# The next pair's first score product placed between two heads' transposes of probabilities

## The chip, the core and the metric

The kernel runs on one core of a Trainium2 chip. The metric is device time in microseconds (us), the median of several runs. The core has TensorE (PE, with its weight loads as PEld), VectorE (DVE), ScalarE (ACT), GpSimd (POOL) and the queue engine SyncE (SP).

## The reference

Attention with sinks and a window (batch 4, 8 heads, 768 positions, head size 64), then a dense layer with a clipped quadratic activation, then an expert-choice layer of 8 experts:

```python
scores = scale * np.matmul(q, k.transpose(0, 1, 3, 2))
keep = is_sink | in_window              # pos < n_sink (4), or 0 <= i - j < window (128)
scores = np.where(keep, scores, -1000000000.0)
scores = scores - np.max(scores, axis=-1, keepdims=True)
a = np.exp(scores)
a = a / (np.sum(a, axis=-1, keepdims=True) + 1e-09)
x = np.matmul(a, v)                     # heads joined: 3072 tokens x 512
...
h = x @ w_in                            # 512 -> 2048
g = np.where(pos, h, np.where(neg, 0.0, (h + beta) ** 2 / (4.0 * beta)))
x = g @ w_out                           # 2048 -> 512
...
logits = x @ w_gate                     # then tokens go to 8 experts of 384 places
out[mask] = np.maximum(x[mask] @ w1[e], 0.0) @ w2[e]
```

Inputs and outputs are float32.

## The kernel before

The 3072 tokens are worked in 12 blocks of 256 (three blocks to a batch entry, so every third one is a "first" block without a block before it). A block's attention is done by pairs of heads, four pairs to a block. Blocks 0 and 1 run in plain float32 (attn_steps_f32); the ten others (attn_steps) split most operands into a high part, rounded to the fast float32 form, and a low part, the remainder.

For a pair of heads the steps are: load_kq and load_v (DMA from SP); trans_k (keys turned on VectorE, the high part ks by ACT on line 303, the low part by VectorE on line 304, columns of the sinks on line 309); trans_q (queries turned on line 431, high part sq by ACT on line 317, low part ql by VectorE on line 318); for each head hh and half u of the block a score product s_hh_u (lines 335 and 336, two products into a PSUM bank; VectorE adds the mask and takes the maximum on line 338, ACT the exponential and its sum on line 340); norm for each head (VectorE sums and reciprocals on lines 345 and 346, GpSimd multiplies the probabilities pr on line 354, or on 349 and 351 in a first block); ptrans for each head (TensorE transposes of the probabilities, line 373, copied out as pt by ACT on 375 and VectorE on 376); strans (the sinks' part of both heads, lines 363 to 366; not in a first block); pv for each head (products with the values, line 392, copied out as xa on 398 and 399); and split (GpSimd, ACT and GpSimd, lines 408 to 413), which writes the pair's quarter of the dense layer's input xh and xl.

ks, sq and ql have one buffer each, so the next pair's can be written only when the last score product of a pair, s11, has read them. Score products, transposes and value products take turns in three PSUM banks.

The order of these steps is a list in `pipeline`: one string per pair, in which a bare name is the pair at hand, "+" the next pair, "*" the one after it, "^" the one after that. `attn` spreads a pair's steps evenly over its time; steps in `idle` take none of it, the others one unit. The dense layer's steps are spread over the same time: hid (12 products of line 634 from xh, xl, then u, gh and gl by lines 642 to 646) and proj (12 products of line 659). `Plan.run` calls all of them in the order of these times, and the Tile scheduler then orders the instructions on each engine: it mostly keeps that order, and moves an instruction behind others that it reckons to be ready sooner. So in TensorE's row a step of 12 products of the dense layer stands between most steps of the attention, and a step that moves in the list moves against these.

After the attention, from about 785 us on, the routing and the experts follow.

Of the kernel before, what the change touches and what calls it, by code (L numbers as in the profile page):

```python
# [74 lines left out]
class Kernel:  # L75
# [524 lines left out]
    def pipeline(self, pairs):  # L600

        idle = {"load_kq", "load_v", "trans_k", "trans_q", "norm0", "norm1", "split_v", "sinks", "split"}

        def steps(order, now, nxt, far, last):
            of = {"": now, "+": nxt, "*": far, "^": last}
            found = [(of[s.rstrip("abcdefghijklmnopqrstuvwxyz_0123456789")], s.lstrip("+*^")) for s in order.split()]
            return [(0.0 if s in idle and s not in d.get("on_pe", ()) else 1.0, d[s]) for d, s in found if d and d[s]]

        out = [steps("load_kq load_v trans_k trans_q +load_kq split_v sinks +load_v s00 s01 norm0 s10 s11 norm1 "
                     "+trans_k +trans_q *load_kq",  # L610
                     pairs[0], pairs[1], pairs[2], None)]
        for now, nxt, far, last in zip(pairs, *(pairs[i:] + [None] * i for i in (1, 2, 3))):
            out.append(steps("ptrans0 ptrans1 strans +s00 +s01 +norm0 pv0 +s10 +s11 +norm1 "
                             "*trans_k *trans_q ^load_kq "
                             "pv1 +split_v +sinks *load_v split", now, nxt, far, last))
        return out
# [765 lines left out]
def tile_sink_window_attention__moe__expert_choice(ctx, tc, q, k, v, n_sink, window, w_in, w_out, wg, w1, w2, out):  # L1382
# [10 lines left out]
    def pipeline(general):  # L1393
        with ExitStack() as c0:
# [72 lines left out]
            plan.run()  # L1467

    pipeline(False)
    flag = nc.values_load(K.flag[0:1, 0:1], min_val=0, max_val=1)  # L1470
    with tc.If(flag):
        with ExitStack() as c0:
            K.attn_general(c0.enter_context, xg)
        pipeline(True)
# [32 lines left out]
```

## Time and profile before

| | us |
|---|---|
| median of 3 runs | 1190.5 (1190.31 to 1192.92) |
| the profiled execution | 1191.5 |
| its span, first to last instruction | 1189.7 |
| TensorE busy | 1113.0 (94%) |
| VectorE busy | 862.4 (72%) |
| ScalarE busy | 701.3 (59%) |
| GpSimd busy | 487.4 (41%) |

Busy shares are averages over stages with different limits. A wait in the trace is the idle time of an engine ahead of an instruction, with what ended it. Products are pipelined and their ends are modelled, so steps on TensorE are best measured from start to start. Times of day are counted from the span's start.

### The profile page before, as it was taken

The numbers are of one execution on the slowest core, as the hardware profiler recorded it, in microseconds if no ns is written. First come the engines' busy times: TensorE is split into PE (matmuls) and PEld (weight loads), VectorE is DVE, ScalarE is ACT, GpSimd is POOL, SyncE is SP. The second block draws the span as 40 slices with busy tenths as digits, with TensorE's granted clock in tenths as the row PEclk, the third lists the DMA queues.
The fourth block names the chain that finished last, engine by engine and source line by source line (L and its number), as shares of the span: only waits on it lengthen the run. The fifth ranks groups of instructions, "written<-read, shape, count | busy, mean of one in ns | idle before, by whom it ended". The sixth has DMA issues, their size and how long they took to land.

```text
span 1189.7 us, 24247 instructions
## 1 busy us (share of the span) xinstructions
PE 1113.0 (94%) x8256; PEld 1027.3 (86%) x8256; DVE 862.4 (72%) x2578; ACT 701.3 (59%) x1602; POOL 487.4 (41%) x588
## 2 busy tenths in 40 slices
PE   5998989999999999999999999999699999999995
PEld 3788878999999999999999999999578888888994
DVE  6778788878677887776778787655788787878330
ACT  5877677666667666666667666642335434443651
POOL 1336645444545445544545554541222222322321
PEclk9999899999999999999999999999799999999998
DMA  4556422323232223222222322000677667666861
GB/s 112 142 163 169 145 51 59 70 42 63 46 63 41 40 54 60 47 46 55 34 57 46 69 46 62 3 19 1 186 196 194 196 169 204 198 191 191 226 177 39
DMA packets 241926, 118.11 MB, mean 99 GB/s; under 512 B 196096, under 2 KB 220672, under 8 KB 241792
## 3 DMA queue, kind: packets, MB, share of 16 engines
q1 hardware_dynamic: 233200, 86.58, 28.5%
q0 software_dynamic: 8592, 29.89, 10.7%
q8 instruction: 67, 1.10, 0.4%
q14 instruction: 67, 0.55, 0.2%
HBM read 86.00 MB, written 13.11 MB: 83 GB/s over the span
## 4 chain that ended last, share of the span: by engine, by line
PE 58%; DVE 13%; issue 10%; ACT 6%; POOL 5%; DMA 4%; SPq 2%; DVEq 0%; POOLq 0%; ACTq 0%
PE hp L634 15%; PE up L659 14%; PE hp L1056 8%; PE us L1083 7%; PE xp L392 2%; PE tp L373 2%; PE sc L335 1%; DVE u L642 1%; PE sc L336 1%; POOL pr L354 1%; SPq L427 1%; DVE ks L304 1%; PE pk L957 1%; ACT u L643 1%; PE sc L517 1%
## 5 line engine op out<-in xcount | busy, mean ns | idle before, releaser
L646 POOL TENSOR_TENSOR gl<-u,gh 128x256 fp32r<-128x256 f32 x192 | 150.8, 785 | 204.6 <-ACT gh L645 163.7
L659 PE MATMUL up<-woh,gl 128*128 128x256 f32 (+1 forms) x576 | 168.5, 293 | 2.9 <-POOL gl L646 2.9
L659 PE MATMUL up<-wol,gh 128*128 128x256 f32 (+1 forms) x576 | 165.5, 288 | 0.8 <-POOL wol L249 0.8
L659 PE MATMUL up<-woh,gh 128*128 128x256 f32 x576 | 164.9, 287 | 0.0
L643 ACT ACTIVATE u<-u,half 128x256 f32<-128x256 f32 x192 | 97.7, 509 | 88.3 <-DVE u L642 84.4
L634 PE MATMUL hp<-xh,wil 128*128 128x256 f32 x768 | 133.5, 293 | 5.2 <-POOL wil L249 3.1
L634 PE MATMUL hp<-xl,wih 128*128 128x256 f32 x768 | 127.3, 286 | 2.6 <-POOL xl L413 2.3
L634 PE MATMUL hp<-xh,wih 128*128 128x256 f32 x768 | 126.2, 285 | 0.0
L634 PEld LDWEIGHTS hp<-xh,wil 128*128 128x128 f32 x768 | 108.3, 192 | 8.8 <-POOL wil L249 4.1
L659 PEld LDWEIGHTS up<-woh,gl 128*128 128x128 f32 x576 | 110.4, 192 | 4.3 <-POOL gl L646 3.7
L659 PEld LDWEIGHTS up<-wol,gh 128*128 128x128 f32 x576 | 110.4, 192 | 1.7 <-POOL wol L249 1.0
L634 PEld LDWEIGHTS hp<-xl,wih 128*128 128x128 f32 x768 | 107.4, 192 | 4.2 <-POOL xl L413 3.8
L659 PEld LDWEIGHTS up<-woh,gh 128*128 128x128 f32 x576 | 110.3, 192 | 0.0
L642 DVE TENSOR_SCALAR u<-hp 128x256 f32<-128x256 f32 x192 | 80.1, 417 | 40.4 <-PE hp L634 32.2
L634 PEld LDWEIGHTS hp<-xh,wih 128*128 128x128 f32 x768 | 107.5, 193 | 0.4 <-issue 0.4
L644 DVE TENSOR_TENSOR u<-hp,u 128x256 f32<-128x256 f32 x192 | 80.6, 420 | 31.8 <-ACT u L643 30.1
L340 ACT ACTIVATE pr<-pr,sm 128x288 f32<-128x288 f32 (+1 forms) x160 | 85.2, 533 | 20.2 <-DVE sm L338 19.7
L354 POOL TENSOR_TENSOR pr<-pr,sm 128x576 f32<-128x576 f32 x56 | 70.0, 1250 | 65.2 <-DVE sm L346 37.3
L645 ACT CAST gh<-u 128x256 fp32r<-128x256 f32 x192 | 77.6, 404 | 27.2 <-DVE u L644 25.0
L1064 ACT ACTIVATE hh<-hp 128x384 fp32r<-128x384 f32 x64 | 31.5, 492 | 104.2 <-PE hp L1056 89.1
L1083 PE MATMUL us<-w2h,hl 128*128 128x512 f32 x192 | 80.8, 421 | 0.0
L376 DVE TENSOR_TENSOR pt<-tp,pt 128x512 fp32r<-128x512 f32 (+1 forms) x80 | 51.4, 647 | 39.6 <-ACT pt L375 39.0
(270 smaller groups left out, 3038.4 us busy)
## 6 DMA issues: line engine op xcount, KB each, us to landing
w1r<-in_moe_w_dram SPq DMA_DIRECT2D x32, 512.0 KB, 4.3
w2r<-in_moe_w_dram SPq DMA_DIRECT2D x32, 512.0 KB, 4.7
w2l<-w2r POOLq DMA_DIRECT2D x32, 512.0 KB
qr<-in_q_dram SPq DMA_DIRECT2D x320, 32.0 KB, 2.0
dr<-in_moe_w_in_dram SPq DMA_DIRECT2D x16, 512.0 KB, 4.1
dr<-in_moe_w_out_dram SPq DMA_DIRECT2D x16, 512.0 KB, 3.7
x2d<-ev SPq DMA_DIRECT2D x26, 256.0 KB, 2.2
kr<-in_k_dram SPq DMA_DIRECT2D x112, 48.0 KB, 2.2
```

Source lines behind the costliest of these rows:

```text
L340: nc.scalar.activation(pr, pr, AF.Exp, bias=sm[:, 0, u:u + 1], scale=-1.0, accum_out=sm[:, 1, u:u + 1])
L354: nc.gpsimd.tensor_tensor(out=pr, in0=pr, in1=r.unsqueeze(2).to_broadcast([P, 2, 2 * P + NS]), op=OP.mult)
L376: nc.vector.tensor_tensor(out=pt[:, 1, :n], in0=ps, in1=pt[:, 0, :n].bitcast(F32), op=OP.subtract)
L634: nc.tensor.matmul(ps, w_[:, k, fs], x_[:, k, :], start=(i == 0 and k == 0), stop=(i == 2 and k == 3))
L642: nc.vector.tensor_scalar(u, ps, -1.0, 1.0, op0=OP.max, op1=OP.min)
L643: nc.scalar.activation(u, u, AF.Square, bias=self.half, scale=0.5)
L644: nc.vector.tensor_tensor(out=u, in0=ps, in1=u, op=OP.max)
L645: nc.scalar.copy(gh, u)
L646: nc.gpsimd.tensor_tensor(out=gl, in0=u, in1=gh.bitcast(F32), op=OP.subtract)
L659: nc.tensor.matmul(o, g_[:, ts], self.w_out_part(w_, f)[:, cs], start=(f == fa and i == 0 and (cs.start > 0 or t == 0)), stop=(f == fz - 1 ...
L1056: nc.tensor.matmul(ps, w_[:, k, fs], x_[:, k, :], start=(i == 0 and k == 0), stop=(i == 2 and k == 3))
L1083: nc.tensor.matmul(us[j], h_[:, o], w_[:, f % 2, :], start=(f == 0 and i == 0), stop=(f == nf - 1 and i == 2))
```

## The change

In the string of every pair, the next pair's first score product (+s00) stands between the first and the second head's transposes. The other steps keep their places.

```diff
         for now, nxt, far, last in zip(pairs, *(pairs[i:] + [None] * i for i in (1, 2, 3))):
-            out.append(steps("ptrans0 ptrans1 strans +s00 +s01 +norm0 pv0 +s10 +s11 +norm1 "
+            out.append(steps("ptrans0 +s00 ptrans1 strans +s01 +norm0 pv0 +s10 +s11 +norm1 "
                              "*trans_k *trans_q ^load_kq "
                              "pv1 +split_v +sinks *load_v split", now, nxt, far, last))
```

What this does to the rows of an engine shows in the built program. TensorE, in a pair of block 7 (its last score product starts at 496.76 us in the trace below); the names are xp for value products, tp for transposed probabilities, hp for the dense layer's hidden products, up for its output products, sc for scores. Before:

```order
L392 MATMUL xp<-pt,v_7047 128x256 x2
L373 MATMUL tp<-ident,pr 128x128 x4
L634 MATMUL hp<-xh,wil 128x256 x4
L634 MATMUL hp<-xl,wih 128x256 x4
L634 MATMUL hp<-xh,wih 128x256 x4
L373 MATMUL tp<-ident,pr 128x128 x4
L659 MATMUL up<-woh,gl 128x256
L659 MATMUL up<-wol,gh 128x256
```

and now:

```order
L392 MATMUL xp<-pt,v_7047 128x256 x2
L373 MATMUL tp<-ident,pr 128x128 x4
L634 MATMUL hp<-xh,wil 128x256 x4
L634 MATMUL hp<-xl,wih 128x256 x4
L634 MATMUL hp<-xh,wih 128x256 x4
L659 MATMUL up<-woh,gl 128x256
L659 MATMUL up<-wol,gh 128x256
L335 MATMUL sc<-ks,ql 128x288
L336 MATMUL sc<-ks,sq 128x288
L659 MATMUL up<-woh,gh 128x256
```

The second head's transposes have left their place behind the hidden products, and the score product stands two output products further on; the transposes follow after the other ten output products of that step.

VectorE, same pair, from the copy of the value products over ql to the copies of the transposes. Before:

```order
L399 TENSOR_TENSOR xa<-xp,xa 64x512
L318 SCALAR_TENSOR_TENSOR ql<-qr,sq 128x512
L376 TENSOR_TENSOR pt<-tp,pt 128x512
L642 TENSOR_SCALAR u<-hp 128x256
L376 TENSOR_TENSOR pt<-tp,pt 128x512
L644 TENSOR_TENSOR u<-hp,u 128x256
L366 TENSOR_TENSOR st<-tps,st 64x256
```

and now:

```order
L399 TENSOR_TENSOR xa<-xp,xa 64x512
L318 SCALAR_TENSOR_TENSOR ql<-qr,sq 128x512
L376 TENSOR_TENSOR pt<-tp,pt 128x512
L642 TENSOR_SCALAR u<-hp 128x256
L338 ISA pr,sm<-sc,m_130 128x288
L338 ISA sm 128x1
L644 TENSOR_TENSOR u<-hp,u 128x256
L376 TENSOR_TENSOR pt<-tp,pt 128x512
```

ql stands where it stood; the mask and maximum of the score product have come ahead of the second head's transposed probabilities.

VectorE in a pair of block 5 (its last score product starts at 376.07 us), around ql. Before:

```order
L304 TENSOR_TENSOR ks<-kr,ks 64x3x128
L399 TENSOR_TENSOR xa<-xp,xa 64x512
L318 SCALAR_TENSOR_TENSOR ql<-qr,sq 128x512
L376 TENSOR_TENSOR pt<-tp,pt 128x512
L642 TENSOR_SCALAR u<-hp 128x256
```

and now:

```order
L304 TENSOR_TENSOR ks<-kr,ks 64x3x128
L346 RECIPROCAL sm<-sm 128x2
L309 CAST ks<-sk 128x2x2x32
L318 SCALAR_TENSOR_TENSOR ql<-qr,sq 128x512
L399 TENSOR_TENSOR xa<-xp,xa 64x512
L642 TENSOR_SCALAR u<-hp 128x256
L376 TENSOR_TENSOR pt<-tp,pt 128x512
```

Here the copy of the value products has moved behind ql.

## Rows read from the trace of the kernel before

**Rows 1.** Sums by stretch: busy us and count by engine, granted clock, DMA.

```profile
150.00:290.00 140.00, 130.85 (x1033) 125.15 (x1032) 113.13 (x314) 96.42 (x248) 70.27 (x87) 1.00 0.27 55
290.00:785.00 495.00, 476.04 (x3875) 470.85 (x3874) 372.03 (x1041) 326.83 (x827) 249.95 (x313) 0.99 0.24 48
```

**Rows 2.** Who TensorE's products waited for, 290 to 785 us (sum, times, longest).

```profile
PE tp L373 <- POOL pr L354: 13.9, 10, 2.0
PE hp L634 <- POOL xl L413: 2.3, 2, 1.2
PE hp L634 <- ACT xh L412: 1.5, 4, 0.5
```

**Rows 3.** The same view, 150 to 290 us.

```profile
PE sc L335 <- DVE ql L318: 2.9, 5, 0.9
PE tp L373 <- POOL pr L354: 2.1, 4, 0.9
```

**Rows 4.** TensorE in order of time: start, us, line, names, count, [idle before].

```profile
496.76 0.29 PE L335 MATMUL sc<-ks,ql 128*128 128x288 f32 x1
497.02 0.28 PE L659 MATMUL up<-woh,gl 128*128 128x256 f32 x1
...
498.46 0.40 PE L392 MATMUL xp<-pt,v 128*128 128x256 f32 x2
...
499.05 0.64 PE L373 MATMUL tp<-ident,pr 128*128 128x128 f32 x4
499.45 0.72 PE L634 MATMUL hp<-xh,wil 128*128 128x256 f32 x4
...
503.02 0.74 PE L373 MATMUL tp<-ident,pr 128*128 128x128 f32 x4 [1.91 <-POOL pr L354]
...
508.23 0.29 PE L335 MATMUL sc<-ks,ql 128*128 128x288 f32 x1
```

**Rows 5.** GpSimd in order of time, same stretch: the second head's normalisation.

```profile
501.50 1.47 POOL L354 TENSOR_TENSOR pr<-pr,sm 128x576 f32<-128x576 f32 x1
```

**Rows 6.** VectorE in order of time, same stretch: up to the low query part.

```profile
500.91 1.04 DVE L304 TENSOR_TENSOR ks<-kr,ks 64x384 fp32r<-64x384 f32 x1
501.99 0.68 DVE L399 TENSOR_TENSOR xa<-xp,xa 64x512 f32<-64x512 f32 x1
502.70 0.81 DVE L318 SCALAR_TENSOR_TENSOR ql<-qr,sq 128x512 fp32r<-128x512 f32 x1
```

**Rows 7.** TensorE in order of time, a pair of a first block.

```profile
436.34 0.30 PE L335 MATMUL sc<-ks,ql 128*128 128x288 f32 x1
...
438.41 0.52 PE L373 MATMUL tp<-ident,pr 128*128 128x128 f32 x3
...
442.22 0.33 PE L335 MATMUL sc<-ks,ql 128*128 128x128 f32 x1
```

**Rows 8.** VectorE in order of time, same pair.

```profile
440.32 1.27 DVE L318 SCALAR_TENSOR_TENSOR ql<-qr,sq 128x512 fp32r<-128x512 f32 x1
```

**Rows 9.** TensorE in order of time, first hidden product of a block.

```profile
469.96 0.39 PE L634 MATMUL hp<-xh,wil 128*128 128x256 f32 x1 [0.43 <-ACT xh L412]
...
471.87 0.38 PE L634 MATMUL hp<-xl,wih 128*128 128x256 f32 x1 [1.17 <-POOL xl L413]
```

**Rows 10.** Sums by stretch, TensorE alone: busy, count, granted clock, DMA, GB/s.

```profile
316.30:319.70 3.40, 3.40 (x19) 0.51 0.43 69
504.00:507.40 3.40, 3.40 (x19) 0.50 0.36 58
570.50:573.90 3.40, 3.40 (x31) 1.00 0.33 52
```

**Rows 11.** Line of the low query part: duration in ns, min/median/max.

```profile
L318 DVE SCALAR_TENSOR_TENSOR ql<-qr,sq x40: 671/694/1791, 103.9 to 752.6; 128x512 fp32r<-128x512 f32 x40
```

**Rows 12.** VectorE in order of time: its first and last row after 285 us.

```profile
285.63 0.68 DVE L318 SCALAR_TENSOR_TENSOR ql<-qr,sq 128x512 fp32r<-128x512 f32 x1
...
752.59 0.81 DVE L318 SCALAR_TENSOR_TENSOR ql<-qr,sq 128x512 fp32r<-128x512 f32 x1
```

## The prediction

> **What bounds the kernel now.** I read the sums by stretch first. From 290 to 785 us, where the attention of the last eight of twelve token blocks runs beside the hidden and output products of the dense layer, TensorE is busy 476 of 495 us at a granted clock of 0.99, and no other engine passes 372 [rows 1]. So in this stretch a wait of TensorE is time lost and little else is. The waits of its products say which: ten waits, 13.9 us, for the normalised probabilities (line 354), another 3.8 us for the attention's output split into xh and xl, and none for the low part of the queries, ql (line 318) [rows 2]. From 150 to 290 us it is the other way round: 2.9 us for ql, 2.1 us for the probabilities [rows 3], and TensorE is less full there. After 785 us no attention is left and the change touches nothing.
>
> The order of time shows where the ten waits are. The last score product of a pair of heads starts at 496.76 us; behind it stand one step of 12 products (497.02 to 498.46, 1.44 us), the value products, the first head's transposes (499.05) and another step of 12; then TensorE stands 1.91 us until 503.02 at the second head's transposes [rows 4]. GpSimd's normalisation of that head starts at 501.50 and takes 1.47 us, to 502.97 [rows 5]. All ten are at the second head's transposes.
>
> **The change part by part.** No instruction is added or removed; the list places the next pair's first score product where the second head's transposes stood, and those (with the sinks') one step later.
>
> *What goes.* In the shown pair the transposes get a step of 12 and the score product more in front of them, about 1.7 us of work, and the normalisation is over meanwhile. Of the ten waits, four lie ahead of the first hidden product of a new block, at most one step of 12 away. Such a product waits for xh and xl itself, as 0.43 and 1.17 us at 469.96 and 471.87 [rows 9]; where it does not, it comes within 0.7 us of it. Its input comes from the pair before by way of DVE, GpSimd, ACT and GpSimd and is no earlier than now; taking the wait ahead of it away lets TensorE reach the next one sooner. I take these four (5.0 us) as worth nothing. Six remain of rows 2, 8.9 us, and a small one of a first block, 0.5. A row counts the idle time only; from arrival to release it is 0.2 us more (arrival in the shown pair: 496.76 + 0.26 + 1.44 + 0.59 + 0.40 + 1.5 = 500.95, release 503.02, so 2.1). Seven waits: 9.4 + 7 x 0.2 = 10.8 us gone.
>
> *What comes.* The score product needs ql, the last link of the next pair's key and query preparation: key parts on ACT and VectorE, the sink columns, queries scaled on ACT, ql on VectorE. None of it can write before the pair's last score product has read the old keys, since there is one buffer. In the shown pair VectorE does the second key part at 500.91, the value output of the head before at 501.99, and ql at 502.70 for 0.81 us, to 503.51 [rows 6]. VectorE and ACT are in nearly the same order in the changed kernel here, so I keep that moment. Today the product comes at 508.23, 4.7 us after ql. Now it stands two products into the step behind the first head's transposes: it is reached at 499.45 + 1.5 + 0.24 = 501.19 and released at 503.57: a new wait of 2.4 us where one of 2.1 was. The chain for ql is as long as the one for the normalisation, because the same crowded VectorE and ACT carry both.
>
> A pair of a first block shows the worse side. Last score product 436.34, first transposes 438.41 [rows 7]; after a step of 12 TensorE would be at the score product at 440.2, but ql runs from 440.32 to 441.59 [rows 8]. It is 442.22 today, no wait; now 1.4 us.
>
> I made this subtraction (end of ql, less the arrival by the new order with 0.12 us a product) for each of the 31 pairs whose ql lies after 285 us (the first and last are in [rows 12]), each counted from the last score product before it. Five places have ql from 5.8 to 6.8 us behind that product while TensorE is there after 4.1 to 4.4 us: 2.4, 2.0, 1.7, 1.6 and 1.4 us. The first-block pair gives 1.5. One (309.57), whose ql has been put behind another output on VectorE, gives between 0.3 and 2.0; I take 1.4. Four give 0.4 to 0.8, together 2.2; four under 0.4, together 1.3. Sum 9.1 + 1.5 + 1.4 + 2.2 + 1.3 = 15.5. Eight have ql 3.6 to 5.5 us after the product and TensorE 5.2 to 5.6 us: no wait. At the eight starts of a block I counted nothing, as above.
>
> Bounds for one new wait: nothing, if ql is always out in time, and 2.5 us (3.8 us of nearest arrival against a ql at 6.3). For the sum: 0 to 24 us (ten like the shown one). I take 15.5, since the same subtraction, made with the normalisation for the old order, finds all ten of rows 2 and only one of note besides.
>
> *The second place of VectorE.* Evictions of the first score product stand ahead of the second head's transposed probabilities; these are not wanted before that head's value products. The sinks' transposes come a step nearer to the first head's value products: 1.85 us in the tightest places where it was 3.6 to 5. Their way over ACT and VectorE took 1.2 to 3 us. That can cost 0 to 1.5 us over all; I take none, because it was long only where VectorE was behind.
>
> *Before 290 us.* Here ql ends a product's time before the score product already [rows 3]. With the list's place alone the five waits of 2.9 us would grow by a step or two each, up to +8 us; but the order puts one to four more steps of the dense layer ahead of the score product in these pairs, and ql moves ahead of other work on VectorE; all waits gone would be -5. I take 0. The first two blocks (float32) have the same new list; what bounds them is weight decoding, taken as 0, within 2 us.
>
> *Clock.* After the 1.91 us wait TensorE's granted clock was 0.50 from 504.0 on: 19 products in 3.4 us, where a stretch at full clock has 31; that is 12 x 0.12 = 1.4 us. The same followed one other wait shown and a third like it, but none of the waits of 1.56 us or less [rows 10]. With new waits near 2.4, 2.2 and 2.0 I expect three or four such drops instead of three: 0, and +3 at most. The Trainium skill (TensorE: Matmul & The Clock Gate, Why this matters for your kernels) lets short gaps pass without loss of clock; by it this term would be nothing in either kernel. The trace differs: the clock did fall after 1.91 us.
>
> ql's line took 671 ns at best, 694 in the median and up to 1791 [rows 11]; 1.27 us of it are in the case above, while GpSimd worked. The Trainium skill (GPSIMD Engine Reference, Key points) says GpSimd shares its SBUF interfaces with VectorE, against instructions with two SBUF inputs, as this one. By that rule the normalisation off the path would still lengthen ql, now on the path; by the bare median the new waits would be some 0.2 us shorter at 11 places, about 2 us less in all.
>
> **Sum.** -10.8 + 15.5 = +4.7 us. The profiled execution took 1191.5 us (span 1189.7 and 1.8 around it): 1196.2. It lies 1.0 above the median of the runs shown, 1190.5; for the median I say 1195.2.
>
> **Rivals.** *The wait shrinks (faster).* Place: the score product of the five short pairs. If ql came 1 us sooner, by one output evicted behind it instead of before it (0.68 us in [rows 6]; the new order does that in one of the five pairs) and less contention, the new waits would be 1.4, 1.0, 0.7, 0.6 and 0.4, the first-block one 0.5, 0.4 at 309.57 and hardly anything elsewhere: 5.0 against 10.8, or 1184.7. It decides at a ql under 5.3 us after the last score product. Against it: the order at the shown pair is unchanged.
>
> *One for one (no change).* Both chains end within 0.6 us of each other in the shown pair. If the nine small and middling new waits vanish, in slack or behind the hidden product's own wait, 15.5 becomes some 11: 1190.7.
>
> *Early part and clock (slower still).* Waits before 290 us grow by half their bound and two more drops of clock: 1195.2 + 4 + 2.8 = 1202.
>
> *The change does not do what it says*: in the early pairs the order does set the score product back behind more of the dense layer. From 290 us on it stands where the list says.
>
> **How the numbers follow.** Forecast 0.45 (own range 1192 to 1199), slower still 0.10, one for one 0.27, faster 0.18. About 0.2%, 2.4 us, is what a measurement of this kernel can tell from no change: 1188.1 to 1192.9. The forecast's lower edge reaches into it, and that of one for one below it: slower 0.53, same 0.28, faster 0.19. The range goes from the faster rival's 1185 to 1201.
>
> **What would show it.** Right: in the waits from 290 us on, the probabilities (line 354) all but vanish and score products waiting for ql appear, 10 to 15 of them, 10 to 14 us; the pair now at 496.76 has 2.2 us there; the first hidden products wait longer for xh and xl than their 3.8 us. Wrong: the ql waits sum to less than 8 us, or ql ends sooner than 5.3 us after the last score product in the short pairs; or the waits are as said and the time is won or lost before 290 us.

## The result and the profile after

| | before | changed |
|---|---|---|
| median, us | 1191.7 (4 runs, 1190.3 to 1193.3) | 1207.8 (4 runs, 1204.4 to 1210.9) |
| ratio, 95% interval | | 1.0134 (1.0101 to 1.0167) |
| the profiled execution, its span | 1191.5, 1189.7 | 1204.4, 1202.6 |
| TensorE busy | 1113.0 | 1114.2 (93%) |
| VectorE, GpSimd busy | 862.4, 487.4 | 863.2, 484.3 |

The change costs 16 us. No engine is busier by more than about 2 us, so the time is idle time of TensorE or slower clock. The profiled execution is the fastest of the four, 12.9 us longer than the one before. The attention's last score product starts at 762.3 us before and 774.9 after; what follows takes as long in both. Of the 12.6 us, 6.0 are lost by the first pair of block 4 (278.6 against 284.7) and 6.6 behind it.

**Behind 290 us.** The sums by stretch, cut close to the same place in the work, with 1838 products of TensorE ahead of the cut before and 1820 after (answers to [rows 1]): columns are the stretch, then busy us and count of PE, PEld, DVE, ACT and POOL, granted clock, DMA share, GB/s.

```profile
150.00:296.00 146.00, 132.54 (x1004) 126.80 (x1003) 108.50 (x307) 95.88 (x247) 68.37 (x85) 0.96 0.25 52
296.00:798.00 502.00, 477.88 (x3897) 470.97 (x3896) 374.92 (x1047) 329.41 (x829) 250.00 (x314) 1.00 0.24 47
```

TensorE is as busy as before in the later stretch, 478 us, but the stretch is 7 us longer. Who its products waited for there (answers to [rows 2]; sum, times, longest):

```profile
PE sc L335 <- DVE ql L318: 15.0, 12, 2.6
PE hp L634 <- ACT xh L412: 5.7, 5, 1.9
PE hp L634 <- POOL xl L413: 1.6, 2, 1.2
PE xp L392 <- DVE st L366: 0.7, 1, 0.7
```

All ten waits for the normalised probabilities are gone; a dozen for ql stand in their place, and the waits for xh and xl have grown from 3.8 to 7.3 us. The pair forecast in detail, TensorE in order of time (answers to [rows 4]; start, us, line, names, count, [idle before]):

```profile
505.84 0.29 PE L335 MATMUL sc<-ks,ql 128*128 128x288 f32 x1
...
508.13 0.65 PE L373 MATMUL tp<-ident,pr 128*128 128x128 f32 x4
508.53 0.72 PE L634 MATMUL hp<-xh,wil 128*128 128x256 f32 x4
...
510.05 0.29 PE L659 MATMUL up<-woh,gl 128*128 128x256 f32 x1
510.17 0.28 PE L659 MATMUL up<-wol,gh 128*128 128x256 f32 x1
512.74 0.40 PE L335 MATMUL sc<-ks,ql 128*128 128x288 f32 x1 [2.29 <-DVE ql L318]
...
514.30 0.52 PE L373 MATMUL tp<-ident,pr 128*128 128x128 f32 x3
```

The score product stands two output products into the next step and waits 2.29 us; it starts 6.90 us after the pair's last score product, where the forecast had 6.81. VectorE, then GpSimd, in the same stretch (answers to [rows 6] and [rows 5]):

```profile
510.08 1.04 DVE L304 TENSOR_TENSOR ks<-kr,ks 64x384 fp32r<-64x384 f32 x1
511.16 0.69 DVE L399 TENSOR_TENSOR xa<-xp,xa 64x512 f32<-64x512 f32 x1
511.87 0.81 DVE L318 SCALAR_TENSOR_TENSOR ql<-qr,sq 128x512 fp32r<-128x512 f32 x1
```

```profile
510.67 1.47 POOL L354 TENSOR_TENSOR pr<-pr,sm 128x576 f32<-128x576 f32 x1
```

VectorE's order is the old one, second key part, value output, ql; ql ends at 512.68. The normalisation ends at 512.14, with 2.2 us to spare until the transposes at 514.30. The pair of a first block (answers to [rows 7] and [rows 8], TensorE, then VectorE):

```profile
443.96 0.30 PE L335 MATMUL sc<-ks,ql 128*128 128x288 f32 x1
...
449.11 0.33 PE L335 MATMUL sc<-ks,ql 128*128 128x128 f32 x1 [1.10 <-DVE ql L318]
```

```profile
447.80 1.26 DVE L318 SCALAR_TENSOR_TENSOR ql<-qr,sq 128x512 fp32r<-128x512 f32 x1
```

It waits 1.10 us, forecast 1.4. The starts of a block were forecast as neutral. Answers to [rows 9]: the product for xl of the same block, and the first product of the next block.

```profile
481.13 0.38 PE L634 MATMUL hp<-xl,wih 128*128 128x256 f32 x1 [1.16 <-POOL xl L413]
545.52 0.39 PE L634 MATMUL hp<-xh,wil 128*128 128x256 f32 x1 [1.92 <-ACT xh L412]
```

The first waits as before; the second, 1.92 us, waited 0.25 us before the change (537.3).

**Before 290 us.** The waits of TensorE's products there (answers to [rows 3]):

```profile
PE sc L335 <- DVE ql L318: 5.2, 6, 1.5
PE gp L219 <- DVE df L247: 2.4, 2, 2.0
PE tp L373 <- POOL pr L349: 1.8, 1, 1.8
```

The new one is gp, a transpose for the gate of the dense layer's weights (line 219), which waits for df (line 247), a decoded part of w_out. SyncE's queue tells why; before, then after (start, us, queue, line, names, count):

```profile
161.63 6.13 SPq L211 DMA_DIRECT2D dr<-in_moe_w_out_dram  x2
170.55 2.02 SPq L427 DMA_DIRECT2D kr<-in_k_dram  x4
172.67 5.36 SPq L427 DMA_DIRECT2D qr<-in_q_dram  x8
```

```profile
161.03 0.34 SPq L211 DMA_DIRECT2D dr<-in_moe_w_out_dram  x1
170.81 1.87 SPq L427 DMA_DIRECT2D kr<-in_k_dram  x4
172.78 5.32 SPq L427 DMA_DIRECT2D qr<-in_q_dram  x8
178.21 0.38 SPq L211 DMA_DIRECT2D dr<-in_moe_w_out_dram  x1
```

The last two loads of w_out's raw weights stand together before (the second issues at 167.4); in the changed kernel the last one stands behind twelve loads of keys and queries and issues at 178.2. Its tile dr has the tag "pr" and so shares two buffers with the probabilities. The plan calls a load at its own time and a step of the attention at its own; the earlier place moves the next pair's first score product from plan time 108.9 to 106.5, and the load stands at 107.25. By the plan's order the score product now claims its buffer first, and the load is left with the one of the pair before. Waiting for that buffer is not what makes it late: the last readers of that pair's probabilities, the transposes of its sinks, are over at 172.8. It is late by its place in the queue, where it issues 0.1 us after the last of the twelve loads (178.10). The plan's order of the two steps decides this, as e3 and e4 show below. The decoding of that part then stands late on VectorE and ScalarE, and TensorE behind it.

### The profile page after: what moved, and what is told of

It reads as the page before. It is cut to its first block, busy times and chain, and to the rows that moved or that the text cites. A ratio compares the mean times of both kernels' runs of the same rounds, so it can differ in the third digit from the quotient of the medians.

```text
span 1202.6 us, 24250 instructions
## 1 busy us (share of the span) xinstructions
PE 1114.2 (93%) x8256; PEld 1028.6 (86%) x8256; DVE 863.2 (72%) x2578; ACT 703.5 (58%) x1602; POOL 484.3 (40%) x588
## 4 chain that ended last, share of the span: by engine, by line
PE 47%; DVE 14%; issue 7%; ACT 5%; DMA 4%; POOL 4%; SPq 2%; DVEq 0%; POOLq 0%; ACTq 0%
PE up L659 12%; PE hp L634 11%; PE hp L1056 8%; PE us L1083 7%; DVE ks L304 2%; SPq L427 2%; PE xp L392 2%; DVE u L642 2%; DVE ql L318 1%; PE tp L373 1%; PE sc L335 1%; DVE qr L431 1%; DMA qr<-in_q_dram 1%; ACT u L643 1%; PE pk L957 1%
## 5 line engine op out<-in xcount | busy, mean ns | idle before, releaser
L646 POOL TENSOR_TENSOR gl<-u,gh 128x256 fp32r<-128x256 f32 x192 | 147.4, 768 | 201.4 <-ACT gh L645 162.6
```

Source lines behind the costliest of these rows:

```text
L646: nc.gpsimd.tensor_tensor(out=gl, in0=u, in1=gh.bitcast(F32), op=OP.subtract)
```

## The experiments

All ran beside the kernel before: 1190.2 (19 runs) for e1 to e4, 1190.9 (29 runs) for e5 to e8, and 1189.7 (29 runs) for e9 to e12, each group on another chip. Intervals are those of the ratio.

A word on the clock first. Each run's record has TensorE's mean granted clock. Over the 192 runs of the 13 kernels here whose clock is on record, a kernel's time falls by 0.73 us for each 0.001 by which its clock is higher, and this alone is 76% of the spread within kernels. So the table has, besides the median, the mean taken to a clock of 0.980 by that slope (the kernel before: 1190.5; standard errors are 0.1 to 0.6 us). This column is an estimate by one slope for all kernels, and no measurement. It is weakest for e9, whose clock lies farthest off: 4.2 of its 5.6 us are the correction, and within its own twelve runs the slope is 0.30.

| kernel | runs | median | ratio | mean clock | at 0.980, against before |
|---|---|---|---|---|---|
| changed, with e5 | 9 | 1207.8 | 1.0153 (1.0127 to 1.0179, e5) | 0.9757 | +14.6 |
| e1 new from block 3 | 4 | 1201.4 | 1.0090 (1.0059 to 1.0121) | 0.9790 | +10.3 |
| e2 new to block 2 | 10 | 1197.4 | 1.0047 (1.0033 to 1.0062) | 0.9768 | +4.2 |
| e3 new, load first | 4 | 1203.0 | 1.0089 (1.0056 to 1.0123) | 0.9777 | +10.4 |
| e4 old, load behind | 10 | 1194.9 | 1.0038 (1.0024 to 1.0051) | 0.9812 | +5.1 |
| e6 old, longer first transposes | 12 | 1183.3 | 0.9954 (0.9936 to 0.9972) | 0.9807 | -5.7 |
| e7 old, sinks' part later | 12 | 1187.6 | 0.9982 (0.9966 to 0.9999) | 0.9820 | -0.7 |
| e8 new, longer first transposes | 12 | 1188.4 | 0.9976 (0.9959 to 0.9994) | 0.9788 | -3.2 |
| e9 new, not at block starts | 12 | 1191.6 | 1.0012 (1.0000 to 1.0025) | 0.9858 | +5.6 |
| e12 new, only at block starts | 12 | 1192.9 | 1.0017 (1.0001 to 1.0033) | 0.9807 | +2.6 |
| e11 new, sq for ql | 6 | 1204.1 | 1.0109 (1.0084 to 1.0134) | 0.9725 | +8.5 |
| e10 e6 and e7 together | 12 | 1189.4 | 0.9987 (0.9967 to 1.0006) | 0.9795 | -1.7 |

A second table takes one profiled execution of each apart, from the last score product of block 4's first pair to that of the last pair. The cost of a stretch at half clock (0.50) is its length less its idle time and less 0.1185 us, about the spacing at full clock, for each product in it. The rest is the products at full clock with the restart after each wait.

| kernel | length | waits | half clock: stretches, cost | rest |
|---|---|---|---|---|
| before | 483.6 | 18.5 | 3, 4.4 | 460.7 |
| changed | 490.2 | 24.9 | 1, 1.5 | 463.8 |
| e5 | 490.0 | 24.8 | 1, 1.5 | 463.7 |
| e1 | 492.4 | 25.2 | 3, 4.6 | 462.7 |
| e2 | 483.5 | 18.9 | 2, 3.0 | 461.6 |
| e3 | 494.4 | 24.9 | 4, 6.1 | 463.4 |
| e4 | 483.2 | 18.7 | 2, 3.2 | 461.3 |
| e7 | 481.6 | 18.5 | 1, 1.5 | 461.5 |
| e9 | 485.3 | 21.3 | 1, 1.5 | 462.5 |
| e12 | 484.2 | 21.9 | 1, 1.5 | 460.8 |
| e11 | 489.3 | 18.8 | 4, 5.4 | 465.1 |
| e6 | 482.6 | 16.2 | 4, 6.2 | 460.2 |
| e8 | 484.5 | 16.6 | 4, 6.2 | 461.7 |
| e10 | 486.7 | 17.8 | 4, 7.3 | 461.6 |

With the clock's cost taken off, e2, e4 and e7, which have the old order in these blocks or nearly so, lie 0.8 to 1.3 us above the kernel before (479.2); differences of that size are not read here. The changed kernel is 9.5 us longer (488.7): 6.4 of it are waits and 3.1 the rest. A wait costs 0.16 us more than its row shows, so five more of them make 0.8 of the 3.1; the other 2.3 are not explained.

**e1 and e2: where in the program.** The new line in the last of the attention's lists only (blocks 3 to 11, e1), or in those before it only (blocks 0, 1 and 2, e2).

```diff
-            out.append(steps("ptrans0 ptrans1 strans +s00 +s01 +norm0 pv0 +s10 +s11 +norm1 "
+            out.append(steps(("ptrans0 +s00 ptrans1 strans " if new else "ptrans0 ptrans1 strans +s00 ")
+                             + "+s01 +norm0 pv0 +s10 +s11 +norm1 "
```

with new = blks[0] >= 3 (e1) or blks[0] < 3 (e2).

> The new order in the last attention list alone (blocks 3 to 11), the old one in blocks 0 to 2. Theory: two separate losses, some 6.5 us from the swapped wait from 285 us on and some 6 us before 285 us from the late last load of w_out; this one keeps the first alone: 1191.7 + 6.5 = 1198, between 1196 and 1201, last load of w_out issued near 167 us, score products waiting for ql 14 to 18 us in all after 285 us. Rival: the steady loss only follows from the early one: 1192, no change.

> The new order in blocks 0 to 2 alone, the old one from block 3 on. Theory: 1191.7 + 6 to 9 = 1198 to 1201, last load of w_out issued near 178 us instead of 167, TensorE some 40 to 50 products behind the kernel before at 290 us, and the waits after 285 us as before (about 14 us for the probabilities). Rival: the early loss comes from the new order in block 3: 1192.

Both parts lose: +11.2 and +7.2 by the medians, together more than the 16 to 17 of the whole change; at equal clock +10.3 and +4.2, together the whole's +14.6. e1 came out just above the range that was expected, e2 just below its own. The change in the early lists is thus a loss of its own. In e2 the last load issues at 178.1 us and the waits from 290 us on are those of the kernel before.

**e3 and e4: the late load alone.** The last part's load planned 1.0 unit earlier in the changed kernel, or 2.0 later in the kernel before.

```diff
-                plan.at(t + TD / 2, lambda f=f: w_out(f))
+                plan.at(t + TD / 2 - (1.0 if f == FT - 1 else 0.0), lambda f=f: w_out(f))   # e3
+                plan.at(t + TD / 2 + (2.0 if f == FT - 1 else 0.0), lambda f=f: w_out(f))   # e4
```

> The new order everywhere, but the step that loads the last part of w_out is planned 1.0 earlier, ahead of the moved score product, so that it takes its buffer (shared with the probabilities) first. Theory: the last load is issued near 167 us again, the early loss goes, the steady one stays: 1198, between 1195 and 1201. Rival: the early loss is the score product's own waiting for ql in blocks 2 and 3: 1204 to 1208 as with the change.

> The old order everywhere, but the step that loads the last part of w_out is planned 2.0 later, behind the next pair's first score product, so that this takes the shared buffer first. Theory: the last load is issued near 178 us, 1191.7 + 4 to 8 = 1196 to 1200, without any change of the list. Rival: the load's moment does not matter: 1192 within 2 us.

With the load back in front (165.9 us), the changed kernel takes 4.8 us less, and at equal clock as much as e1 (+10.4 and +10.3): the early part of the change costs nothing but the late load. The old order with the late load takes 4.7 us more. Its queue and its wait:

```profile
167.91 2.02 SPq L427 DMA_DIRECT2D kr<-in_k_dram  x4
170.04 4.91 SPq L427 DMA_DIRECT2D qr<-in_q_dram  x8
175.07 0.38 SPq L211 DMA_DIRECT2D dr<-in_moe_w_out_dram  x1
```

```profile
181.92 0.63 PE L219 MATMUL gp<-ident,df 128*128 128x128 f32 x4 [1.37 <-DVE df L247]
```

It is the same picture as in the changed kernel, with no step of the attention moved. Neither time lay in its expected range: e3 is 2 us above, 1 short of its rival, and e4 is 1 us below, 1 beyond its rival. What speaks against the rivals is that the four runs of e3 (1199.0 to 1205.2) lie below eight of the nine of the changed kernel (1204.4, then 1206.6 to 1211.1), and that e4's interval excludes 1.

**e5: the changed kernel again.**

> The changed kernel once more, for more runs and a second trace. Theory: the instructions and waits are the same each time, and what differs from run to run is how often the clock falls; so the time of a run goes down by 0.7 to 1.3 us for each 0.001 that its mean granted clock is higher, and the waits for ql from 290 to 800 us are again 15 to 18 us. Median 1205 to 1209. Rival: the spread is in the waits themselves, these then differ by 3 us or more from the first trace.

1207.8 (1206.6 to 1211.1, 5 runs). The second trace has the same waits from 290 to 800 us, 16.3 us for ql against 16.5, and the same length of the stretch in the second table; its span is 6.6 us longer, 6.4 of it before 240 us, where 37.5 us are at half clock against 20.4 in the first trace. So these two traces differ by the clock and not by the waits for ql.

**e9 and e12: starts of a block against the other pairs.** The new line from block 3 on, in all pairs of a block but the first (e9), or in the first alone (e12), the one whose transposes stand ahead of a new block's first hidden product.

```diff
+            new = len(pairs) > 8 and i_ % 4 != 0     # e9; e12: i_ % 4 == 0
```

> The new order from block 3 on, except in the one pair of each block whose transposes stand ahead of the first hidden product of a new block; there the old order. Theory (the block starts, taken as worth nothing in the prediction, cost about 3 us in the new order): 1201.4 of the kernel with the new order in all pairs from block 3 on, less 3, is 1198; from 290 to 800 us ql waits of 11 to 13 us, the normalisation's 4 to 5 us at block starts, and xh and xl back at about 4 us. Rival (the block starts are neutral and the loss is all in the other pairs): 1201 or more.

> The other half: the new order from block 3 on only in the one pair of each block that stands ahead of a new block's first hidden product. Theory: 1190.9 + 3 = 1194; there the waits for the normalisation (5.0 us) go, one or two for ql (4 us) and 3.5 us more for xh and xl come. Rival (neutral, as the prediction took it): 1189 to 1192.

TensorE's waits from 290 to 800 us, e9, then e12 (hidden products are on line 636 there):

```profile
PE sc L335 <- DVE ql L318: 11.3, 10, 2.1
PE tp L373 <- POOL pr L354: 5.0, 4, 2.6
PE hp L636 <- POOL xl L413: 2.3, 2, 1.2
PE hp L636 <- ACT xh L412: 1.9, 4, 0.8
```

```profile
PE tp L373 <- POOL pr L354: 9.1, 6, 2.0
PE hp L636 <- ACT xh L412: 3.9, 4, 2.0
PE sc L335 <- DVE ql L318: 3.6, 3, 1.9
PE hp L636 <- POOL xl L413: 2.8, 3, 1.2
```

The waits are as the theory had them. The starts are not neutral, and e12's median lies between the theory's 1194 and the rival's 1189 to 1192: in e12 the normalisation's waits there (13.9 less 9.1) went, and 3.6 for ql (1.6 more at 286.8, ahead of this window) and 2.9 more for xh and xl came; with the clock's part taken off, its stretch is 3.5 us longer (482.7 against 479.2). e9's is 4.6 longer (483.8). Its median came out far below the expected 1198, only 1.9 us above the kernel before. Its clock is the highest of all kernels, 0.9858, with no stretch at half clock before 290 us in its trace and one from there to the attention's end; why is not shown. In the traces the two add up to nearly the whole, 3.5 + 4.6 = 8.1 against e1's 8.6; at equal clock to 8.2 of 10.3, where e1 has four runs.

**e11: no ql in the first score product.**

```diff
-                nc.tensor.matmul(ps[:, o], st["ql"][:, hh, u, :], k, start=True, stop=False)
+                nc.tensor.matmul(ps[:, o], st["sq" if u == hh == 0 else "ql"][:, hh, u, :], k, start=True, stop=False)
```

> The changed kernel, but the first score product of every pair multiplies the high part sq twice instead of the low part ql and then sq: the low part of the queries is left out there, with as many products as before. Theory (the wait for ql is the loss from 290 us on): the 16.5 us of ql waits there go; where sq on ScalarE is late too some 3 to 5 us of waits for sq remain (in the trace of the changed kernel sq ends 1.35, 0.71, 0.66 and 0.38 us after TensorE's arrival in four pairs), and the late load before 190 us stays: 1207.8 - 12 = 1196, range 1193 to 1199. Rival (ql is only the last of several late things; sq, the keys' copies or the hidden products' inputs take over): 1202 or more.

```profile
PE hp L634 <- ACT xh L412: 7.6, 6, 1.9
PE sc L335 <- ACT sq L317: 6.1, 8, 3.0
PE xp L392 <- DVE st L366: 2.7, 5, 0.7
PE hp L634 <- POOL xl L413: 1.4, 2, 1.2
```

The first score products lack the low part of the queries here, so this kernel only serves to find the cause. By its time, 1204.1, it is the rival's case, but its clock is the lowest of all (0.9725); by its waits it lies between the two theories. The 16.5 us of ql went, and 9.8 came back: 6.1 for sq, in twice the places that its end in the changed kernel's trace had suggested, 1.7 more for xh and xl, 2.0 more for the sinks' transposes, which now stand close ahead of the value products. TensorE reaches each next place sooner and waits there. At equal clock it gains 6.1 us of the 14.6, in its trace 4.8 of the 9.5. So ql is the last of several links that end nearly together; taking it away is worth little more than a third of its row.

**e8 and e6: time instead of place.** The first head's transposes take two units of the pair's time instead of one, in the new order (e8) and in the old (e6); one step of 12 products more stands behind them.

```diff
-            return [(0.0 if s in idle and s not in d.get("on_pe", ()) else 1.0, d[s]) for d, s in found if d and d[s]]
+            return [(0.0 if s in idle and s not in d.get("on_pe", ()) else 2.0 if s == "ptrans0" else 1.0, d[s]) for d, s in found if d and d[s]]
```

> The new order, with the first head's transposes given two units of time, so that the score product is reached one step of the dense layer (1.5 us) later; the last load of w_out's raw weights stands ahead of the next pair's probabilities as in the kernel before. Theory: the five long waits for ql of 2.4 to 1.4 us shrink by 1.5 each and the small ones go, as no wait for the normalisation comes back; waits for ql from 290 to 800 us at most 5 us, and without the late load 1187 to 1193. Rival: the place is not what matters, VectorE has become the bound through the new order, and ql comes later by as much: waits as in the changed kernel, 1198 to 1203.

> The old order, but the first head's transposes are given two units of the pair's time instead of one, so that one step of the dense layer more stands ahead of the second head's transposes. Theory (the place behind the first head's transposes is reached too early for either chain; the score product further on is reached late enough): the ten waits for the normalised probabilities go, no waits for ql come in their place, and the four at block starts turn into waits for xh or xl; 1190.2 - 5.8 = 1184, range 1181 to 1188. Rival: the step taken from elsewhere in the pair opens the same wait there (at the score product or the value products): 1190 or more.

Waits from 290 to 800 us, e8, then e6:

```profile
PE hp L634 <- ACT xh L412: 10.0, 7, 2.1
PE hp L634 <- POOL xl L413: 4.2, 5, 1.2
PE sc L335 <- DVE ql L318: 1.6, 2, 1.0
```

```profile
PE hp L634 <- ACT xh L412: 10.7, 7, 2.9
PE hp L634 <- POOL xl L413: 4.1, 5, 1.2
PE tp L373 <- POOL pr L354: 0.2, 1, 0.2
```

Both times came out in the ranges expected. In e8 ql's waits fall to 1.6 us, and the load stands in front again, by the new spacing. e6 beats both kernels: 1183.3, 7.5 us under the kernel before. Neither chain is late there, but most of the time that its waits took is waited elsewhere: 13.7 of the normalisation's 13.9 us went, and at the starts of blocks the waits for xh and xl grew from 3.8 to 14.8. From block 4 on its stretch is 2.8 us shorter with the clock's cost taken off (476.4 against 479.2). In the profiled executions 7.2 of the 8.2 us that e6 gains lie before that, where the kernel before had three stretches at half clock and e6 none. So the removed waits are shown for those 2.8 us; what makes the rest of the gain is not shown.

**e7 and e10: the sinks' transposes.** The next pair's first score product between the second head's transposes and the sinks', in the old order (e7) and with e6's longer step (e10).

```diff
-            out.append(steps("ptrans0 ptrans1 strans +s00 +s01 +norm0 pv0 +s10 +s11 +norm1 "
+            out.append(steps("ptrans0 ptrans1 +s00 strans +s01 +norm0 pv0 +s10 +s11 +norm1 "
```

> The old order, but the next pair's first score product stands between the second head's transposes and those of the sinks. This is the one part of the change (the sinks' transposes a step later, the score product a little earlier) without the other (the score product ahead of the second head's transposes). Theory: the loss sits in the score product taking the early place; here it stays behind the second head's transposes, the ten waits for the normalisation stay as they are, ql is out in time: 1189 to 1193. Rival: the sinks' transposes, nearer to the first head's value products, cost part of the steady loss: 1194 or more, with waits at the value products.

> The old order with two units for the first head's transposes, and besides the next pair's first score product ahead of the sinks' transposes (but behind the second head's). Each alone gave 1183.3 and 1187.6 against 1190.9. Theory: the first gains by taking the waits for the normalisation away, the second by letting the score product and its evictions start a little sooner, so they add up in part: 1178 to 1182. Rival: both gain in the same place (before 285 us, where the traces of both are early), then 1183 again.

e7: the ten waits for the normalisation stay (12.3 us), none for ql comes, and at equal clock it is the kernel before within 0.7 us; its median is a little better than expected, with a clock of 0.9820. So the loss is the score product's place ahead of the second head's transposes, not the sinks'. e10 lost most of what e6 had won, against both expectations. One wait is new in it:

```profile
PE xp L392 <- DVE st L366: 2.7, 5, 1.1
```

The value products wait five times for the sinks' part, as in e11. That is 2.7 us of some 4; the rest is not shown.

## Why the prediction was wrong

The direction was right, and so was the mechanism from 290 us on except at the starts of blocks; 1207.8 lies outside the range of 1185 to 1201, 12.6 us above the forecast.

- *What goes*: right. All ten waits of [rows 2] went.
- *What comes*: right. Ten waits for ql outside the starts of a block sum to 12.0 us in the changed kernel (16.5 less 2.56, 1.49 and 0.43 at starts), or some 14 with the 0.2 us that a row leaves out each; forecast 15.5. The shown pair came to 0.1 us. Other places did less well, and the sum is in part luck: the five long waits were forecast at 9.1 us and gave 5.9 in four places (2.29, 1.22, 1.18 and 1.18), while two others gave more, 1.69 where 1.4 was taken and 1.47 where at most 0.8 was. The fifth is the pair of block 5 at 376.07, whose VectorE order had changed: ql ended 6.42 us after the last score product there, and 4.29 in the changed kernel, so no wait came. The part that these two terms forecast as +4.7 is e9: +4.6 in the trace without the clock's part, +5.6 by the runs at equal clock, +1.9 by the medians as they are.
- *"At the eight starts of a block I counted nothing"*: wrong. Four waits, 5.0 us in all, went there; 4.5 for ql and 3.5 more for xh and xl came. The score product, with ql's wait, now stands ahead of the hidden product, and the pair's output that this needs is no earlier. e12: +2.6 at equal clock, +3.5 in its trace.
- *"Before 290 us ... I take 0"*: the step that failed. It looked at ql's waits and at bounds of -5 to +8 for them, and the loss came from elsewhere: a DMA that shares buffers with the probabilities came to stand behind the moved product. No row of TensorE's waits before shows it; the order of SyncE's queue, before and after, does. At equal clock the late load costs 4.2 us in e2 and 5.1 in e4, and e3 takes it back.
- *The second place of VectorE*: taken as none, with 1.5 as its bound. One value product waited 0.7 us for the sinks' part.
- *Clock*: taken as 0, with +3 as its bound. Runs of the changed kernel have 0.9757, of the kernel before 0.9801: 3.2 us. But not as predicted: from 290 us on there was one stretch at half clock, not three or four; the others lie before 290 us, one of them behind the wait for the late load.

Together, by the estimates at equal clock: 4.7 became about 5.6, 2.6 at the starts, 2 of e1 that these two leave open, 4.2 for the load, 3.2 of clock: 17.6, against 17.9 between the means of all runs and 16 to 17 between the medians. What stays open is why the clock falls as often as it does in one kernel and not in another (e9), and those 2 us.

## What to carry to other kernels

A step that is moved in a list also moves when its buffers are claimed: compare the order of the DMA queue, not only that of the compute engines, and look for tiles with the same tag. Where two chains end within a microsecond of each other, exchanging their consumers exchanges one wait for another; spacing (more independent work behind the step both hang on, e6) took both away here, though most of that time then came back as waits at the starts of blocks. And before a difference of a few us between kernels is explained by their waits, take the mean granted clock of the runs into account, and look in the trace for where the time was gained or lost.

## What the runs showed of the hardware

The traces give no rule for the granted clock by the length of a wait. In the changed kernel it fell to 0.50 (the lower of its two levels, 1.2 of 2.4 GHz) behind the wait of 2.56 us (667.1) and, at 186.8, behind that of 1.99 us (184.5), and stayed at 1.00 behind the one of 2.29 us (sums by stretch, TensorE alone, answers to [rows 10]: busy, count, granted clock, DMA, GB/s):

```profile
668.10:671.50 3.40, 3.40 (x18) 0.50 0.41 66
512.70:516.10 3.40, 3.36 (x27) 1.00 0.50 81
186.80:190.20 3.40, 3.40 (x17) 0.50 0.00 0
```

e9 had waits of 2.06 and 2.55 us, with no fall behind either, and one fall, to 0.50 from 471.2 us, behind a wait of 1.16 us (470.52). The kernel before had a wait of 1.17 us at the same place, and its clock stayed at 1.00; so the prediction's reading that no fall follows a wait of 1.56 us or less holds for the trace it was taken from and not for this one. The Trainium skill (TensorE: Matmul & The Clock Gate, Why this matters for your kernels) lets short gaps pass without loss of clock; the trace agrees behind the 2.29 us and differs behind the 1.99 us, so length alone does not decide here. Behind the wait for the late load (1.4 to 2.4 us) the clock fell within 3 us in all five traces that have that load, and in none of the nine others between 180 and 200 us. Over all runs, 0.001 of the mean granted clock goes with 0.73 us of this kernel.

ql's own duration did not change (answers to [rows 11]; min/median/max ns), though it now stands where TensorE waits for it:

```profile
L318 DVE SCALAR_TENSOR_TENSOR ql<-qr,sq x40: 670/694/1541, 94.5 to 764.9; 128x512 fp32r<-128x512 f32 x40
```
